# Strassen form for one batch more, work moved between batches, and weight loads reordered, in a fused attention and feed-forward kernel

## The chip, the cores and the metric

One core of one Trainium2 chip. The metric is device time in microseconds (us); a time below is the median of several executions, with the lowest and highest in brackets. Executions whose granted TensorE clock and length mark them as slow are left out of every ratio. TensorE multiplies matrices; VectorE, ScalarE and GpSimd work on vectors. In the profile they are PE, DVE, ACT and POOL. SBUF and PSUM are memories on the chip: in this program TensorE's results go into banks of PSUM, and a bank is copied out before TensorE uses it again.

## The reference, cut to what matters

```
x: 8 batches, 8 heads, 512 rows, 64 wide      state: 8, 8, 32, 64
a     = softmax(x state^T / 8);   xread = a state
a2    = softmax(state x^T / 8);   sread = a2 x
y     = concat(xread, sread), heads side by side       # 8 x 544 rows of 512
h     = y @ w_in                                       # 512 -> 2048
g     = 0.5 h (1 + erf(h / sqrt 2))
out   = g @ w_out                                      # 2048 -> 512
```

The last two products, 512 rows per batch, are nearly all of the time. For the rows of xread the kernel never forms y: it folds state and w_in into one matrix P per batch, so that h = a P.

## The kernel before

First, batch by batch, TensorE forms P (`p_mm`), the first product (`mm1`, called through `M`) and the second. The second has two forms. The plain one (`mm2`, through `U`, and `mm2_m`) is 64 matmuls of 512 columns. The Strassen form (`X`) is seven products of 16 matmuls of 256 columns, and it needs sums of quarters of w_out, made once, and sums of quarters of g, made per batch. Before the change batches 0 and 1 take the plain form.

```
def p_mm(b, f, tiles):                  # one quarter of P, two PSUM banks
    ps = [tiles([128, 512], "p_ps") for t in range(2)]
    ...
def p_copy(b, f, ps):
    nc.scalar.copy(out=dst[:, 0, :], in_=ps[0])
    nc.vector.tensor_copy(out=dst[:, 1, :], in_=ps[1])

def evac(ps, rows):                     # an output tile leaves its bank
    nc.vector.tensor_copy(out=osb, in_=ps)
    ...
```

Second, VectorE's operations with two inputs in SBUF: the multiply that normalises the softmax, the sums of w_out and the sums of g.

```
    nc.vector.tensor_tensor(out=A.a[...], in0=e4, in1=ics[...], op=ALU.mult)      # norm
    nc.vector.tensor_tensor(out=w_sum[name], in0=x, in1=y, op=op)                # w_add
    nc.vector.tensor_tensor(out=t, in0=g_q(b, h0, k0), in1=g_q(b, h1, k1), op=op) # g_sum
```

Third, the weights come in four chunks each of w_in and w_out, counted from 0. After the first ones the queue holds, in this order, w_out 1, w_in 2, w_out 2, w_in 3, w_out 3, and then x of the later batches.

The softmax here doesn't subtract the row's maximum and nothing guards it: scores larger than these inputs give would overflow.

Of the kernel before, what the change touches and what calls it, by code (L numbers as in the profile page):

```python
# [17 lines left out]
def kernel(  # L18
# [8 lines left out]
    nc = tc.nc  # L27

    B, H, S, D = x.shape
    _, _, NS, _ = state.shape  # L30
# [6 lines left out]
    FC = d_ff // 512  # L37
# [41 lines left out]
    hold = persist.tile([128, 1], BF16, name="hold")  # L79
# [23 lines left out]
    def load_w_in(f0, f1):  # L103
        for t in range(2):
            nc.gpsimd.dma_start(
                out=w_in_bf[64 * t:64 * t + 64, :, f0:f1],
                in_=moe_w_in[256 * t:256 * t + 256, f0:f1].rearrange("(c d) f -> d c f", c=HC),
            )
# [3 lines left out]
    def load_w_out(i):  # L112
        nc.gpsimd.dma_start(out=w_out_bf[:, 4 * i:4 * i + 4, :], in_=w_out_r[:, 4 * i:4 * i + 4, :])

    def load_x(b):
        xb = xin.tile([128, H, SJ * D], BF16, name="xb", tag="xb")
        nc.gpsimd.dma_start(out=xb, in_=xr[b])
        xbs[b] = xb
# [12 lines left out]


    def load_rest():
        load_w_out(1)
        for f in range(2, FC):
            load_w_in(512 * f, 512 * f + 512)
            load_w_out(f)
        load_st(2, B)
        load_x(2)
        load_x(3)  # L140


# [80 lines left out]
    def rearr_ones(b):  # L223
        A = atts[b]
        eng = nc.vector if b < 2 else nc.gpsimd
        src = xbs[b].rearrange("p (t c) (j d) -> p t c j d", t=2, d=D)
        for t in range(2):
            eng.tensor_copy(  # L228
                out=A.xo[:, :, :, 2 + 64 * t:66 + 64 * t].rearrange("p j c d -> p c j d"),
                in_=src[:, t],  # L230
            )
# [122 lines left out]
    def atr(b, ts=(0, 1)):  # L354
        A = atts[b]
        if 0 in ts:
            A.AT = att.tile([128, SJ, 2, 128], BF16, name="AT", tag="AT")
        for t in ts:
            ps = ps_f.tile([128, SJ, 128], BF16, name="aT_ps", tag="f")
            for j in range(SJ):  # L360
                nc.tensor.transpose(ps[:, j, :], A.a[:, 2 * j + t, :], ident)
            nc.vector.tensor_copy(out=A.AT[:, :, t, :], in_=ps)
# [36 lines left out]
    def srt(b):  # L399
        A = atts[b]  # L400
        ps = ps_f.tile([128, HC, NS], BF16, name="srT", tag="f")
        nc.tensor.transpose(
            ps.rearrange("p c n -> p (c n)"), A.srm.rearrange("q t d -> q (t d)"), ident
        )
        nc.vector.tensor_copy(out=XSR[:, :, :, b], in_=ps)
# [3 lines left out]
    def p_mm(b, f, tiles):  # L409
        if b not in Ps:  # L410
            Ps[b] = att.tile([128, 2, d_ff], BF16, name="P", tag="P")
        ps = [tiles([128, 512], "p_ps") for t in range(2)]
        for c in range(HC):
            for t in range(2):
                nc.tensor.matmul(  # L415
                    ps[t][32 * c:32 * c + 32, :],
                    lhsT=sbd[64 * t:64 * t + 64, b, c, 32 * t:32 * t + 32],
                    rhs=w_in_bf[64 * t:64 * t + 64, c, f * 512:(f + 1) * 512],
                    start=True,
                    stop=True,  # L420
                )
        return ps

    def p_copy(b, f, ps):
        dst = Ps[b][:, :, f * 512:(f + 1) * 512]
        nc.scalar.copy(out=dst[:, 0, :], in_=ps[0])  # L426
        nc.vector.tensor_copy(out=dst[:, 1, :], in_=ps[1])  # L427

    def pmat(b, f):
        p_copy(b, f, p_mm(b, f, ftile))  # L430



# [1 line left out]
    def burst(chunks, b_read=None):  # L435
        done = []
        first = len(chunks) < 4 and b_read is not None
        if first:
            sread(b_read)
        for i, (b, f) in enumerate(chunks):  # L440
            done.append((b, f, p_mm(b, f, ftile if i < 2 else otile)))
        for x in done[:2]:
            p_copy(*x)
        if b_read is not None and not first:
            sread(b_read)
        for x in done[2:3]:
            p_copy(*x)
        if b_read is not None:
            sread_out(b_read)
        for x in done[3:]:  # L450
            p_copy(*x)
# [19 lines left out]
    gs = {}  # L471
# [73 lines left out]
    def mm2_m(b, m):  # L545
        for j in range(SJ):
            if m == 0:
                ops[b, j] = otile([128, d_model], "op")
            nc.tensor.matmul(  # L549
                ops[b, j],  # L550
                lhsT=gs[b][:, m, j * 128:(j + 1) * 128],
                rhs=w_out_bf[:, m, :],
                start=(m == 0),
                stop=(m == MC - 1),
            )
# [5 lines left out]
    w_sum = {}  # L561

    def w_add(name, x, y, op):
        if name == "3":
            pair = persist.tile([128, 2, MH, NH], BF16, name="ws_34", tag="mix0")
            w_sum["3"], w_sum["4"] = pair[:, 0], pair[:, 1]
        elif name != "4":
            tag = {"6": "mix1", "1": "mix2", "7": "mix3"}[name]
            w_sum[name] = persist.tile([128, MH, NH], BF16, name=f"ws_{name}", tag=tag)
        nc.vector.tensor_tensor(out=w_sum[name], in0=x, in1=y, op=op)  # L570

    def w_sums(i):
        (b11, b12), (b21, b22) = w_q
# [120 lines left out]
    def M(*ms):  # L694
        for m in ms:
            mm1(m // MC, m % MC)

    def U(*us):
        for u in us:
            mm2(u // 16, u % 16 // 4, u % 4)  # L700
# [69 lines left out]
    scores(1, 0)  # L770
    scores(1, 1)
    srt(0)
    U(4, 5)
    rearr_ones(1)
    U(6)
    pmat(0, 2)
    norm(1, 0)
    norm(1, 1)
    U(7)
# [1 line left out]
    sread(1)  # L781
    sread_out(1)
    M(10, 11)
    mm2_m(0, 8)
    mm2_m(0, 9)
    burst([(0, 3), (1, 0)])
    mm2_m(0, 10)
    atr(1)
    M(12, 13)
    srt(1)  # L790
    M(14, 15)
    mm2_m(0, 11)
    begin(2)
    rearr(2)
    xtr_dma(2)
    rearr_ones(2)
    U(12)
    burst([(1, 1), (1, 2)])
    U(13)
    state_prep(2, B)  # L800
    M(16, 17)
    U(14)
    M(18, 19)
    U(15)
    burst([(1, 3), (2, 0), (2, 1)])
    U(16)


    u = 17
    for p in range(2, 8):  # L810
        if p == 4:
            scores(2, 0)
            scores(2, 1)
            norm(2, 0)
            norm(2, 1)
        if p == 7:
            atr_dma(2)
        if p == 3:
            begin(3)
            rearr(3)  # L820
            xtr_dma(3)
            rearr_ones(3)
        M(16 + 2 * p, 17 + 2 * p)
        U(u)
        u += 1
        if p in (5, 7):
            pmat(2, 2 + p // 7)
        if p >= 3:
            w_sums(p - 3)
        if p == 2:  # L830
            nc.gpsimd.tensor_copy(out=hold, in_=gs[1][:, 4, 0:1])
            load_x(4)

    for b in range(2, B):
        nb = b + 1
        for p in range(8):
            k = 16 * b + 2 * p
            if p == 1 and nb < B:
                scores(nb, 0)
                scores(nb, 1)  # L840
            if p in (2, 3) and nb < B:
                norm(nb, p - 2)
            if p == 3 and nb + 1 < B:
                xtr_dma(nb + 1)
            if p == 5 and nb < B:
                atr_dma(nb)
            M(k, k + 1)
            if p == 2:
                srt(b)
            if nb == B and p >= 4:  # L850
                for m in range(4 * p - 16, 4 * p - 12):
                    mm1_sr(m)
            if b == 2:
                for _ in range(2 if p < 4 else 1):
                    if u < 32:
                        U(u)
                        u += 1
            elif p < 5:
                if p == 0:
                    g_sum(b - 1, "5")  # L860
                X(b - 1, "45127"[p])
                if p < 3:
                    g_sum(b - 1, "127"[p])
            if p == 1:
                sread(b)
                sread_out(b)
            if p == 0 and b + 3 < B:
                nc.gpsimd.tensor_copy(out=hold, in_=gs[b][:, 0, 0:1])  # L868
                load_x(b + 3)
            if p == 0 and nb + 1 < B:  # L870
                begin(nb + 1)
                rearr(nb + 1)
            if p == 2 and nb + 1 < B:
                rearr_ones(nb + 1)
            if p == 5:
                g_sum(b, "6")
                if nb < B:
                    p_run(nb, (0, 1), ((0, 1), (3, 2)))
            if p == 6:
                X(b, "3")  # L880
            if p == 7:
                if nb < B:
                    p_run(nb, (2, 3), ((1, 2), None))
                X(b, "6")
# [46 lines left out]
```

## Time and profile before

| | before |
|---|---|
| time | 212.62 us (212.35 to 212.8) |
| profiled span | 211.0 us |
| TensorE busy | 201.6 us, 96% |
| first product of batch 2 starts | 55.68 us |
| first product of batch 3 starts | 76.17 us |

The two starts serve as milestones: all of the change lies before the second one. In timelines each line has start, length, engine, source line, operation, output<-inputs, and in brackets the idle time before it and what ended that. These are the milestones, and the row of the page that gives the granted TensorE clock in 40 slices of the span (9 is full). The clock never drops.

```profile
55.68 1.04 PE L478 MATMUL hp<-AT,P 128*128 128x512 bf16 x4
...
76.17 1.03 PE L478 MATMUL hp<-AT,P 128*128 128x512 bf16 x4
```
```profile
PEclk9999999999999999999999999999999999999999
```

### The profile page before, as it was taken

How to read it: one execution, taken by the hardware profiler on the slowest of the kernel's cores; microseconds unless marked ns; L12 is line 12 of the kernel's file. 1: busy time of each engine (PE TensorE's matmuls, PEld its weight loads, DVE VectorE, ACT ScalarE, POOL GpSimd, SP SyncE). 2: the span in 40 equal slices, each digit the busy share in tenths (PEclk: the TensorE clock that was granted, in tenths of full speed). 3: DMA queues.
4: the chain of work that ended last, by engine and by line, in shares of the span. 5: the costliest groups of instructions: out<-in, count | busy, mean ns of one | idle time of the engine just before them, and what ended most of it. 6: DMA issues, size and time to landing. Idle time of an engine off the chain costs nothing.

```text
span 211.0 us, 4598 instructions
## 1 busy us (share of the span) xinstructions
PE 201.6 (96%) x1929; PEld 128.8 (61%) x1939; DVE 133.6 (63%) x206; ACT 131.2 (62%) x237; POOL 64.1 (30%) x71
## 2 busy tenths in 40 slices
PE   7899999998999999999999999999999999999991
PEld 7645444443454576766675677567766778786860
DVE  2934575748829549984899658955875571324521
ACT  3864775679794779467947596678758455860110
POOL 8954302573171025610566007200230022000320
PEclk9999999999999999999999999999999999999999
DMA  6999999779274909355872910160007001300314
GB/s 201 189 170 204 206 194 186 158 173 179 50 99 102 249 0 127 77 199 53 111 90 122 198 31 3 57 193 3 2 22 230 3 0 47 155 0 0 103 68 132
DMA packets 37861, 23.14 MB, mean 110 GB/s; under 512 B 21712, under 2 KB 35280, under 8 KB 37840
## 3 DMA queue, kind: packets, MB, share of 16 engines
q0 software_dynamic: 13936, 8.10, 28.0%
q1 hardware_dynamic: 23216, 14.29, 27.6%
q10 hardware_dynamic: 688, 0.46, 0.7%
q8 instruction: 15, 0.25, 0.5%
q14 instruction: 6, 0.05, 0.1%
HBM read 17.30 MB, written 8.91 MB: 124 GB/s over the span
## 4 chain that ended last, share of the span: by engine, by line
PE 79%; DMA 10%; DVE 5%; ACT 3%; issue 1%; POOL 0%; ACTq 0%
PE xp L602 32%; PE hp L478 22%; PE op L504 9%; DMA w_out_bf<-in_moe_w_out_dram 6%; PE p_ps L415 4%; DVE gsum L596 3%; PE hps L519 3%; PE ops L531 3%; DMA AT<-a 3%; PE op L549 2%; DMA st_f<-in_state_dram 2%; PE sr L378 1%; PE xT_ps L250 1%; PE pt L324 1%; ACT g L485 1%; DVE s L645 1%
## 5 line engine op out<-in xcount | busy, mean ns | idle before, releaser
L485 ACT ACTIVATE g<-hp 128x512 bf16<-128x512 f32 x124 | 67.5, 603 | 33.7 <-PE hp L478 28.6
L478 PE MATMUL hp<-AT,P 128*128 128x512 bf16 x248 | 63.9, 380 | 0.3
L602 PEld LDWEIGHTS <-gsum 128*128 128x128 bf16 x480 | 46.3, 98 | 11.0 <-issue 2.1
L596 DVE TENSOR_TENSOR gsum<-g 128x2048 bf16<-128x2048 bf16 x30 | 40.0, 1349 | 7.9 <-ACT g L485 6.8
L478 PEld LDWEIGHTS <-P 128*128 128x128 bf16 x248 | 22.4, 98 | 20.7 <-issue 2.6
L602 PE MATMUL xp<-ws,gsum 128*128 128x256 bf16 x288 | 34.4, 273 | 0.0
L427 DVE CAST P<-p_ps 128x512 bf16<-128x512 f32 x31 | 20.0, 684 | 17.2 <-PE p_ps L415 17.2
L650 POOL TENSOR_TENSOR u<-s,oh 128x512 f32<-128x512 f32 x6 | 8.0, 1329 | 67.8 <-ACT oh L648 67.8
L504 PE MATMUL op<-w_out_bf,g 128*128 128x512 bf16 x90 | 23.0, 379 | 0.6 <-DMA w_out_bf<-in_moe_w_out_dram 0.4
L602 PE MATMUL xp<-ws,g 128*128 128x256 bf16 x192 | 22.9, 273 | 0.0
L602 PE MATMUL xp<-w_out_bf,gsum 128*128 128x256 bf16 x192 | 22.9, 273 | 0.0
L426 ACT CAST P<-p_ps 128x512 bf16<-128x512 f32 x31 | 17.0, 604 | 7.4 <-PE p_ps L415 7.4
L602 PEld LDWEIGHTS <-g 128*128 128x128 bf16 x192 | 18.8, 98 | 4.3
L504 PEld LDWEIGHTS <-g 128*128 128x128 bf16 x96 | 9.1, 98 | 11.8 <-issue 1.6
L218 POOL COPY x<-xb 128x1024 bf16<-128x1024 bf16 x12 | 12.6, 1082 | 10.9 <-DMA xb<-in_x_dram 10.9
L347 DVE TENSOR_TENSOR a<-e,ics 128x512 bf16<-128x512 bf16 x14 | 15.1, 1078 | 0.5
L228 POOL COPY xo<-xb 128x1024 bf16<-128x1024 bf16 x12 | 13.5, 1157 | 1.3 <-PE sr L378 1.3
L645 DVE TENSOR_TENSOR s<-xp,s 128x512 f32<-128x512 f32 x6 | 4.2, 692 | 14.5 <-PE xp L602 14.5
L621 POOL TENSOR_TENSOR v<-q,oh 128x512 f32<-128x512 f32 x6 | 8.0, 1326 | 15.8 <-ACT oh L652 13.8
L344 DVE TENSOR_REDUCE cs<-e 128x16 f32<-128x512 bf16 x14 | 9.5, 677 | 3.8 <-ACT e L331 3.8
L415 PE MATMUL p_ps<-w_in_bf,sbd 64*32 64x512 bf16 x248 | 11.0, 383 | 0.8 <-ACT g L485 0.7
L868 POOL COPY hold<-g 128x1 bf16<-128x1 bf16 x3 | 1.0, 330 | 31.0 <-ACT g L485 31.0
(91 smaller groups left out, 208.4 us busy)
## 6 DMA issues: line engine op xcount, KB each, us to landing
out_dram<-oh SPq DMA_DIRECT2D x11, 512.0 KB, 2.7
xb<-in_x_dram POOLq DMA_DIRECT2D x7, 512.0 KB, 6.9
out_dram<-osb SPq DMA_DIRECT2D x9, 256.0 KB, 3.3
w_out_bf<-in_moe_w_out_dram POOLq DMA_DIRECT2D x4, 512.0 KB, 12.6
w_in_bf<-in_moe_w_in_dram POOLq DMA_DIRECT2D x6, 256.0 KB, 12.2
x0f<-in_x_dram SPq DMA_DIRECT2D x3, 256.0 KB, 4.0
w_in_bf<-in_moe_w_in_dram POOLq DMA_DIRECT2D x4, 128.0 KB, 3.9
x0f<-in_x_dram ACTq DMA_DIRECT2D x1, 256.0 KB, 4.4
```

What stands on the lines that cost most here:

```text
L218: nc.gpsimd.tensor_copy(out=A.x4[:, :, :, 64 * t:64 * t + 64].rearrange("p j c d -> p c j d"), in_=src[:, t],)
L228: eng.tensor_copy(out=A.xo[:, :, :, 2 + 64 * t:66 + 64 * t].rearrange("p j c d -> p c j d"), in_=src[:, t],)
L344: nc.vector.reduce_sum(out=cs, in_=e4, axis=AX.X)
L347: nc.vector.tensor_tensor(out=A.a[:, :, hs].rearrange("p g (c n) -> p g c n", n=NS), in0=e4, in1=ics[:, :, :].to_broadcast((128, G, 2, NS) ...
L415: nc.tensor.matmul(ps[t][32 * c:32 * c + 32, :], lhsT=sbd[64 * t:64 * t + 64, b, c, 32 * t:32 * t + 32], rhs=w_in_bf[64 * t:64 * t + 64, c ...
L426: nc.scalar.copy(out=dst[:, 0, :], in_=ps[0])
L427: nc.vector.tensor_copy(out=dst[:, 1, :], in_=ps[1])
L478: nc.tensor.matmul(hp, lhsT=Ps[b][:, t, m * 128:(m + 1) * 128], rhs=atts[b].AT[:, :, t, :], start=(t == 0), stop=(t == 1),)
L485: nc.scalar.activation(out=gs[b][:, m, :], in_=hp, func=AF.Gelu)
L504: nc.tensor.matmul(ps, lhsT=gs[b][:, m, j * 128:(j + 1) * 128], rhs=w_out_bf[:, m, :], start=(m == 0), stop=(m == MC - 1),)
L596: nc.vector.tensor_tensor(out=t, in0=g_q(b, h0, k0), in1=g_q(b, h1, k1), op=op)
L602: nc.tensor.matmul(ps[:, j - js[0], :], lhsT=lhs[:, m, 128 * j:128 * j + 128], rhs=rhs[:, m, :], start=(first and j == js[0] and m == 0), ...
```

## The change

Its intent: give batch 1 the cheaper Strassen form; fill the gaps that this leaves by moving half of batch 0's second product back among batch 1's first; and bring w_in one chunk ahead of w_out. With more sums to make on VectorE, three of the five sums of w_out go to GpSimd. Batch 0's third P product also moves ahead of three steps of its second product, with both of its copies on VectorE. The core of the diff (`atr` transposes the normalised attention on TensorE, `atr_dma` by DMA; `srt` transposes sread):

```
 def load_rest():
+    load_w_in(1024, 1536)
     load_w_out(1)
-    for f in range(2, FC): load_w_in(512 * f, 512 * f + 512); load_w_out(f)
+    load_w_in(1536, 2048)
+    load_w_out(2)
     load_st(2, B); load_x(2)
+    load_w_out(3)
     load_x(3)
 def w_add(name, x, y, op):
+    eng = nc.vector if name in "36" else nc.gpsimd
-    nc.vector.tensor_tensor(out=w_sum[name], in0=x, in1=y, op=op)
+    eng.tensor_tensor(out=w_sum[name], in0=x, in1=y, op=op)
 ... (the stretch around batch 1 is written anew; its end:)
+    scores(2, 0); scores(2, 1)
+    w_sums(0); w_sums(1)               # "3" on VectorE, "4" on GpSimd
+    nc.gpsimd.tensor_copy(out=hold, in_=gs[1][:, 4, 0:1]); load_x(4)
+    M(24, 25)
+    U(14)
+    norm(2, 0); norm(2, 1)
+    U(15)                              # its output copy is behind both norms
+    w_sums(2); w_sums(3); w_sums(4)    # "6" on VectorE, "1" and "7" on GpSimd
+    M(26, 27)
+    g_sum(1, "6")
+    p_run(2, (0, 1), ((0, 1), (3, 2))) # P in the banks of batch 0's output
+    M(28, 29); X(1, "3"); M(30, 31)
+    atr(2)                             # was atr_dma(2)
+    p_run(2, (2, 3), ((1, 2), None))
+    X(1, "6")
 for b in range(2, B): ...
+    if p == 3: srt(b)
     M(k, k + 1)
-    if p == 2: srt(b)
-    if b == 2: U(...)                  # batch 1's plain second product
+    if p < 5: ... X(b - 1, "45127"[p])
```

More of the change, by code (lines that the diff above doesn't have):

```diff
@@ L133, in load_rest @@
     def load_rest():
+        load_w_in(1024, 1536)
         load_w_out(1)
-        for f in range(2, FC):
-            load_w_in(512 * f, 512 * f + 512)
-            load_w_out(f)
+        load_w_in(1536, 2048)
+        load_w_out(2)
         load_st(2, B)
         load_x(2)
+        load_w_out(3)
         load_x(3)
@@ L422, in p_mm, with p_copy, pmat @@
         return ps
-    def p_copy(b, f, ps):
+    def p_copy(b, f, ps, first=None):
         dst = Ps[b][:, :, f * 512:(f + 1) * 512]
-        nc.scalar.copy(out=dst[:, 0, :], in_=ps[0])
+        (first or nc.scalar.copy)(out=dst[:, 0, :], in_=ps[0])
         nc.vector.tensor_copy(out=dst[:, 1, :], in_=ps[1])
-    def pmat(b, f):
-        p_copy(b, f, p_mm(b, f, ftile))
+    def pmat(b, f, first=None):
+        p_copy(b, f, p_mm(b, f, ftile), first)
     def burst(chunks, b_read=None):
@@ L772 @@
     srt(0)
+    pmat(0, 2, nc.vector.tensor_copy)
     U(4, 5)
@@ L775 @@
     U(6)
-    pmat(0, 2)
     norm(1, 0)
@@ L783 @@
     M(10, 11)
+    burst([(0, 3), (1, 0)])
+    M(12, 13)
+    atr(1)
+    M(14, 15)
     mm2_m(0, 8)
+    srt(1)
     mm2_m(0, 9)
-    burst([(0, 3), (1, 0)])
-    mm2_m(0, 10)
-    atr(1)
-    M(12, 13)
-    srt(1)
-    M(14, 15)
-    mm2_m(0, 11)
+    burst([(1, 1), (1, 2)])
     begin(2)
@@ L796 @@
     rearr_ones(2)
+    M(16, 17)
+    mm2_m(0, 10)
+    M(18, 19)
+    mm2_m(0, 11)
+    state_prep(2, B)
+    pmat(1, 3)
+    begin(3)
+    rearr(3)
+    xtr_dma(3)
+    rearr_ones(3)
+    M(20, 21)
     U(12)
-    burst([(1, 1), (1, 2)])
+    M(22, 23)
     U(13)
-    state_prep(2, B)
-    M(16, 17)
+    scores(2, 0)
+    scores(2, 1)
+    w_sums(0)
+    w_sums(1)
+    nc.gpsimd.tensor_copy(out=hold, in_=gs[1][:, 4, 0:1])
+    load_x(4)
+    M(24, 25)
     U(14)
-    M(18, 19)
+    norm(2, 0)
+    norm(2, 1)
     U(15)
-    burst([(1, 3), (2, 0), (2, 1)])
-    U(16)
-    u = 17
-    for p in range(2, 8):
-        if p == 4:
-            scores(2, 0)
-            scores(2, 1)
-            norm(2, 0)
-            norm(2, 1)
-        if p == 7:
-            atr_dma(2)
-        if p == 3:
-            begin(3)
-            rearr(3)
-            xtr_dma(3)
-            rearr_ones(3)
-        M(16 + 2 * p, 17 + 2 * p)
-        U(u)
-        u += 1
-        if p in (5, 7):
-            pmat(2, 2 + p // 7)
-        if p >= 3:
-            w_sums(p - 3)
-        if p == 2:
-            nc.gpsimd.tensor_copy(out=hold, in_=gs[1][:, 4, 0:1])
-            load_x(4)
+    w_sums(2)
+    w_sums(3)
+    w_sums(4)
+    M(26, 27)
+    g_sum(1, "6")
+    p_run(2, (0, 1), ((0, 1), (3, 2)))
+    M(28, 29)
+    X(1, "3")
+    M(30, 31)
+    atr(2)
+    p_run(2, (2, 3), ((1, 2), None))
+    X(1, "6")
     for b in range(2, B):
@@ L846 @@
                 atr_dma(nb)
+            if p == 3:
+                srt(b)
             M(k, k + 1)
-            if p == 2:
-                srt(b)
             if nb == B and p >= 4:
@@ L852 @@
                     mm1_sr(m)
-            if b == 2:
-                for _ in range(2 if p < 4 else 1):
-                    if u < 32:
-                        U(u)
-                        u += 1
-            elif p < 5:
+            if p < 5:
                 if p == 0:
```

## The prediction

> **What bounds the kernel now.** I read the page first (busy time, then the chain), then TensorE in order of time, then the waits, then VectorE and GpSimd side by side.
>
> ```profile
> PE 201.6 (96%) x1929; PEld 128.8 (61%) x1939; DVE 133.6 (63%) x206; ACT 131.2 (62%) x237; POOL 64.1 (30%) x71
> PE 79%; DMA 10%; DVE 5%; ACT 3%; issue 1%; POOL 0%; ACTq 0%
> ```
>
> TensorE sets the time: 96% busy, so of 211.0 us only 9.4 are open, of which about 1 lies at the start and about 4 after the last matmul. What another order can win is therefore small. The waits of TensorE, all of them:
>
> ```profile
> PE srT L402 <- DVE srm L392: 0.8, 2, 0.4
> PE p_ps L415 <- ACT g L485: 0.7, 1, 0.7
> PE aT_ps L361 <- POOL a L309: 0.5, 1, 0.5
> PE op L504 <- DMA w_out_bf<-in_moe_w_out_dram: 0.4, 1, 0.4
> PE op L549 <- DMA w_out_bf<-in_moe_w_out_dram: 0.3, 1, 0.3
> ```
>
> The loads are barely ahead early on. In the timeline (start, length, engine, line, idle before in brackets) the second chunk of w_out is met as it lands, and the piece of the chain below gives its landing, 10.16 + 11.90 = 22.06. By the issue-to-landing times of their line, the two halves of w_in's third chunk (issued from 10.97) land at about 22.8 and 24.2.
>
> ```profile
> 10.16 11.90 DMA w_out_bf<-in_moe_w_out_dram
> 22.10 2.75 PE L504 MATMUL op<-w_out_bf,g 128*128 128x512 bf16 x11 [0.36 <-DMA w_out_bf<-in_moe_w_out_dram]
> 24.78 0.41 PE L415 MATMUL p_ps<-w_in_bf,sbd 64*32 64x512 bf16 x8
> 25.12 1.04 PE L504 MATMUL op<-w_out_bf,g 128*128 128x512 bf16 x4
> ```
>
> Most telling for this change is VectorE beside GpSimd. The same multiply (softmax normalisation, both inputs in SBUF) takes 0.69 us while GpSimd rests and 1.45 to 1.57 us while it works:
>
> ```profile
> 50.96 0.69 DVE L347 TENSOR_TENSOR a<-e,ics 128x512 bf16<-128x512 bf16 x1
> 83.33 1.26 POOL L650 TENSOR_TENSOR u<-s,oh 128x512 f32<-128x512 f32 x1 [2.31 <-ACT oh L648]
> 84.55 2.49 POOL L228 COPY xo<-xb 128x1024 bf16<-128x1024 bf16 x2
> 84.56 1.57 DVE L347 TENSOR_TENSOR a<-e,ics 128x512 bf16<-128x512 bf16 x1
> 88.99 1.27 POOL L621 TENSOR_TENSOR v<-q,oh 128x512 f32<-128x512 f32 x1 [1.96 <-ACT oh L652]
> 89.36 1.45 DVE L347 TENSOR_TENSOR a<-e,ics 128x512 bf16<-128x512 bf16 x1
> ```
>
> The last pair shows the size of it: GpSimd ends at 90.26, the multiply at 90.81, so it ran only about 0.6 us after GpSimd let go.
>
> **What the Trainium skill says.** "SBUF — State Buffer", section "Who interferes with whom": a VectorE instruction with two SBUF inputs and a GpSimd instruction that reads SBUF exclude each other, the second waiting until the first has finished. The trace agrees, up to the 1.27 us of its longest GpSimd arithmetic. "GPSIMD Engine Reference", section 3.1: tensor_tensor on GpSimd costs about 2.6 cycles per element. At that page's 1.2 GHz, 512 elements are 1.1 us; the trace has 1.27 for u. "TensorE: Matmul & The Clock Gate", Part 1: after some 3.4 us of idling TensorE runs at half clock until it has been busy as long again. No wait in this trace is long enough to show that.
>
> **The change, part by part.**
>
> *Strassen for batch 1.* Removed: 64 matmuls of 512 columns. From start to start the trace has 0.864 us per four (24.78 to 26.00 less the 0.34 of the eight small ones), so 13.8 us. Added: 112 matmuls of 256 columns, 1.745 us per 16 (the chain has 1.75), so 12.2. Gain 1.6. But the transpose of batch 2's attention moves from the DMA queue to TensorE: eight transposes, +0.45 (31.48 to 31.93). Net -1.2 us on TensorE.
>
> *Old waits that go.* The srT transposes move behind a Strassen product: two waits, 0.8 us, gone. The copy that frees their PSUM bank now stands behind a later normalisation, which may return some; I count -0.5. The 0.7 us wait on ScalarE, plus slack around it (TensorE advances by less than its work between 47 and 52), and the 0.36 on w_out sit in stretches I rebuild below; from 22.1 to the first product of batch 3 (76.17) I count about 1.6 us idle before.
>
> *Loads.* w_in chunk 3 and w_out chunk 2 only swap places in a queue that is never empty there, so their sum lands at the same 24.15. TensorE now does the small products of w_in's chunk first (21.7 to about 22.5) and then needs w_out: it waits from about 22.5 to 24.2, **+1.7**. Later chunks are early enough.
>
> *Back to back.* Batch 1's first product now follows the P bursts with nothing between; it must wait for the copies of P out of PSUM (0.6 to 0.7 us each on ScalarE and VectorE). Three such places, about **+1.3** together.
>
> *A bank held by VectorE.* The built program shows that the second P product of batch 2 needs the bank of batch 0's last output tile, and the copy that empties it stands on VectorE behind both normalisations of batch 2. I estimate that TensorE is there at about 48.2 to 48.6. The normalisations can't start before the exponentials: scores at 44.2, and in the trace 2.4 us from the scores to the first reduction, then the output copy in front, so 47.1. In the trace both take 48.35 to 51.57, 3.2 us; plus 0.6 for the copy gives 51. So even with GpSimd at rest: **+2.5**.
>
> *Three weight sums to GpSimd.* Each is 128x2048, on VectorE 1.22 us. On GpSimd I scale u: 4 x 1.27 = 5 at most, and the page's 2.6 cycles give 4.4; I use 4.4. They stand in a row, 13 us, from when x of batch 3 has been loaded and rearranged, which my count of the loads puts at about 43, until about 58. In just that stretch VectorE has five operations with two SBUF inputs to do, in order: sum 3, two normalising multiplies, sum 6, the first difference of g. Sum 3, ready at 44.9, waits to 47; done 48.3. Then osb copy, reduction, reciprocal (1.6 us together) and the multiply meets GpSimd's second sum, which started at about 49.7: it waits to 54.2. The second multiply meets the third sum: to 58.6 or 59.3. Only then is the bank emptied, at about 60. If the first multiply wins its race (both come within 0.3 us of each other) the bank is free at 56, but sum 6 then waits out the third GpSimd sum and the P copies behind it come as late as 63. Either way batch 2's first product starts at about 66.5, not 57.8 as without the exclusion: **+8.5**. A wait that long would also cool the clock: an estimate from the page, 3.4 us at half rate, is **+1.7**.
>
> Sum: without exclusion -1.2 - 1.6 - 0.5 + 1.7 + 1.3 + 2.5 = +2.2, with some 0.5 for later copies +2.7: **215.3**. With it +2.7 + 8.5 + 1.7 = +12.9: **225.5**. After batch 2 both kernels run the same stages and nothing is won back, as TensorE is full there.
>
> **Rivals.**
> 1. *The mild one:* GpSimd yields inside a long instruction, or its sums run earlier, and only the bank wait and the load wait remain: 213 to 217. For it: the trace shows the exclusion only with instructions of up to 1.3 us. Against it: at every overlap I looked at, the multiply ended as though it had begun when GpSimd ended.
> 2. *The intended one:* order and loads fit, all waits in the early stretch vanish. TensorE's 1.2 us, 1.6 us of old waits and 0.5 of srT are all there is: 209.3. Against it: the load wait and the bank wait follow from the program's order and from landings that the trace gives. For it: someone who moves so many things presumably looked at where they fell.
> 3. *The harsh one:* exclusion, a cold clock, and delays that carry into batch 2's VectorE work, where three more differences of g queue: 226 to 229.
>
> **Range and chances.** I hold the exclusion more likely than not (about 0.6), and the mild and intended cases 0.4 together, so my number lies between the modes, nearer the upper one: 221.5. The range spans both: 212.5 to 228. More than 2% faster would need 4.3 us where at most 3.3 are to be had: 0.03. Slower by over 2% is above 216.9: 0.59. Within: 0.38.
>
> **What would show it.** TensorE's waits: one on w_out near 22 of about 1.7 us (loads); one of a P product of batch 2 on VectorE's output copy near 48, 2.5 us (mild) or 8 to 12 (exclusion). On VectorE: the L347 multiply of batch 2 (a line or so further down) at several us each, and the sum beside it, ending where a GpSimd sum ends; 0.69 each would refute the exclusion. On GpSimd: three tensor_tensor of 4 to 5 us. The granted clock just after the wait shows the cooling. The prediction fails if GpSimd's sums take 2 us, or if they come before or after VectorE's chain.

## The result, and the profile after

The changed kernel takes 225.72 us (224.93 to 226.56, four runs) against 212.71 us (212.35 to 213.52) of the kernel before on the same chip: 13.0 us slower. The ratio is 1.061 (95% interval 1.055 to 1.066). Ratios here are the mean time of one kernel's fast runs over that of the other's in the same rounds, so not quite the ratio of the medians.

The profiled span is 224.3 us. Three views say where the time went. The page's busy line, chain and clock row:

```profile
PE 203.3 (91%) x1989; PEld 134.8 (60%) x1995; DVE 147.3 (66%) x211; ACT 132.7 (59%) x239; POOL 79.9 (36%) x76
PEclk9999999997589999999999999999999999999999
PE 61%; DVE 23%; DMA 10%; issue 2%; POOL 1%; ACT 1%; SPq 0%; DVEq 0%
```

VectorE's share of the chain that ended last is 23%, where it was 5%, and the clock has a hole near a quarter of the span. TensorE's waits (total, times, longest):

```profile
PE p_ps L416 <- DVE osb L492: 10.7, 1, 10.7
...
PE op L505 <- DMA w_out_bf<-in_moe_w_out_dram: 0.8, 1, 0.8
...
PE p_ps L416 <- DVE XSR L406: 0.4, 1, 0.4
```

One wait of 10.7 us is most of the loss of 13.0. Now TensorE in order of time, at the load wait and around the long one:

```profile
22.39 0.41 PE L416 MATMUL p_ps<-w_in_bf,sbd 64*32 64x512 bf16 x7 [0.43 <-DVE XSR L406]
23.63 3.61 PE L505 MATMUL op<-w_out_bf,g 128*128 128x512 bf16 x15 [0.83 <-DMA w_out_bf<-in_moe_w_out_dram]
...
59.56 0.62 PE L416 MATMUL p_ps<-w_in_bf,sbd 64*32 64x512 bf16 x7 [10.73 <-DVE osb L492]
60.12 1.89 PE L479 MATMUL hp<-AT,P 128*128 128x512 bf16 x4
61.80 2.57 PE L604 MATMUL xp<-ws,g 128*128 128x256 bf16 x16
64.21 1.03 PE L479 MATMUL hp<-AT,P 128*128 128x512 bf16 x4
...
68.13 1.03 PE L479 MATMUL hp<-AT,P 128*128 128x512 bf16 x4
...
90.26 1.03 PE L479 MATMUL hp<-AT,P 128*128 128x512 bf16 x4
```

The second P product of batch 2 waits from 48.83 to 59.56 for an output copy on VectorE. Then four matmuls take 1.68 us from start to start (0.864 at full rate) and the Strassen product behind them 2.41 (1.745): the clock was cold, at a cost of about 1.5 us. Batch 2 starts at 68.13, 12.45 later than before; batch 3 at 90.26, 14.09 later. From there to the end 134.0 us pass against 134.8. What held VectorE is seen beside GpSimd:

```profile
44.89 2.88 DVE L572 TENSOR_TENSOR ws<-w_out_bf 128x2048 bf16<-128x2048 bf16 x1
...
49.28 8.02 DVE L348 TENSOR_TENSOR a<-e,ics 128x512 bf16<-128x512 bf16 x1
...
58.22 0.69 DVE L348 TENSOR_TENSOR a<-e,ics 128x512 bf16<-128x512 bf16 x1
58.83 0.68 DVE L492 COPY osb<-op 128x512 f32<-128x512 f32 x1
```
```profile
42.62 4.06 POOL L572 TENSOR_TENSOR ws<-w_out_bf 128x2048 bf16<-128x2048 bf16 x1
46.63 1.18 POOL L816 COPY hold<-g 128x1 bf16<-128x1 bf16 x1
47.75 0.91 POOL L117 DMA_DIRECT2D xb<-in_x_dram  x1
48.68 8.06 POOL L572 TENSOR_TENSOR ws<-w_out_bf 128x2048 bf16<-128x2048 bf16 x2
```

GpSimd's first sum ends at 46.68, and VectorE's sum 3, waiting since 44.89, ends 1.09 later, which is about its own length. In that time GpSimd's copy of one column takes 1.18 instead of 0.18: here GpSimd waited for VectorE. Then the multiply waits through both of GpSimd's next sums: they end at 56.74, the multiply at 57.30. The second multiply, with GpSimd at rest, takes 0.69.

### The profile page after: what moved, and what is told of

It reads as the page before. It is cut to its first block, busy times and chain, and to the rows that moved or that the text cites. A ratio compares the mean times of both kernels' runs of the same rounds, so it can differ in the third digit from the quotient of the medians.

```text
span 224.3 us, 4723 instructions
## 1 busy us (share of the span) xinstructions
PE 203.3 (91%) x1989; PEld 134.8 (60%) x1995; DVE 147.3 (66%) x211; ACT 132.7 (59%) x239; POOL 79.9 (36%) x76
## 3 DMA queue, kind: packets, MB, share of 16 engines
HBM read 17.30 MB, written 8.91 MB: 117 GB/s over the span
## 4 chain that ended last, share of the span: by engine, by line
PE 61%; DVE 23%; DMA 10%; issue 2%; POOL 1%; ACT 1%; SPq 0%; DVEq 0%
PE xp L604 28%; PE hp L479 17%; DVE gsum L598 7%; DVE a L348 7%; DMA w_out_bf<-in_moe_w_out_dram 5%; PE p_ps L416 4%; PE hps L520 3%; PE ops L532 3%; DMA AT<-a 3%; PE op L505 2%; DVE cs L345 2%; DMA x0f<-in_x_dram 2%; PE op L550 2%; DVE ws L572 1%; DVE ics L347 1%
## 5 line engine op out<-in xcount | busy, mean ns | idle before, releaser
L604 PEld LDWEIGHTS <-gsum 128*128 128x128 bf16 x560 | 54.3, 98 | 13.9 <-issue 2.3
L598 DVE TENSOR_TENSOR gsum<-g 128x2048 bf16<-128x2048 bf16 x35 | 46.8, 1353 | 7.9 <-ACT g L486 6.8
L604 PE MATMUL xp<-ws,gsum 128*128 128x256 bf16 x336 | 40.2, 273 | 0.0
L604 PE MATMUL xp<-ws,g 128*128 128x256 bf16 x224 | 27.4, 277 | 0.0
L604 PE MATMUL xp<-w_out_bf,gsum 128*128 128x256 bf16 x224 | 26.7, 273 | 0.0
L604 PEld LDWEIGHTS <-g 128*128 128x128 bf16 x224 | 22.3, 100 | 5.7 <-issue 0.5
L427 ACT CAST P<-p_ps 128x512 bf16<-128x512 f32 x30 | 16.5, 601 | 13.9 <-PE p_ps L416 13.8
L416 PE MATMUL p_ps<-w_in_bf,sbd 64*32 64x512 bf16 x248 | 12.8, 389 | 11.3 <-DVE osb L492 10.7
L348 DVE TENSOR_TENSOR a<-e,ics 128x512 bf16<-128x512 bf16 x14 | 22.5, 1605 | 0.5
L416 PEld LDWEIGHTS <-sbd 64*32 64x32 bf16 x248 | 3.1, 89 | 20.7 <-issue 20.4
L572 POOL TENSOR_TENSOR ws<-w_out_bf 128x2048 bf16<-128x2048 bf16 x3 | 12.1, 4054 | 0.0
L654 ACT COPY oh<-xp 128x512 f32<-128x512 f32 x7 | 4.1, 587 | 10.0 <-PE xp L604 4.0
```

Source lines behind the costliest of these rows:

```text
L348: nc.vector.tensor_tensor(out=A.a[:, :, hs].rearrange("p g (c n) -> p g c n", n=NS), in0=e4, in1=ics[:, :, :].to_broadcast((128, G, 2, NS) ...
L416: nc.tensor.matmul(ps[t][32 * c:32 * c + 32, :], lhsT=sbd[64 * t:64 * t + 64, b, c, 32 * t:32 * t + 32], rhs=w_in_bf[64 * t:64 * t + 64, c ...
L427: (first or nc.scalar.copy)(out=dst[:, 0, :], in_=ps[0])
L572: eng.tensor_tensor(out=w_sum[name], in0=x, in1=y, op=op)
L604: nc.tensor.matmul(ps[:, j - js[0], :], lhsT=lhs[:, m, 128 * j:128 * j + 128], rhs=rhs[:, m, :], start=(first and j == js[0] and m == 0), ...
```

## The experiments

The theory: most of the loss is VectorE shut out while GpSimd's sums run (called the exclusion), reaching TensorE through the output copy behind the multiplies; the rest is the bank wait that is there anyway, the cold clock and the load wait. The main rivals: the order on VectorE alone causes it, or the early loads do. There were twelve runs of eleven kernels, all with correct results.

**sums_vector: all five sums on VectorE.**

```
-        eng = nc.vector if name in "36" else nc.gpsimd
+        eng = nc.vector
```

> The changed kernel with all five weight sums on VectorE, nothing else. Theory (exclusion between GpSimd's long sums and VectorE's two-input work): the 8 us multiply falls back to 0.69 us, the wait of the P product on the output copy shrinks from 10.7 to about 3 us (the order of VectorE's program alone), a second wait of about 1.5 us appears at the next P products because the copies of P stand behind three more sums; batch 2's first product starts at about 60 instead of 68.1, total about 217.5. Rival (the order of the copy alone, GpSimd innocent): VectorE gets more work, so the wait does not shrink and the time stays at 225 or grows.

Measured: 218.97 us (217.95 to 220.83), ratio 1.030 (1.023 to 1.036). Having the three sums on GpSimd rather than on VectorE therefore costs about 6.8 of the 13.0 us, by the medians. The first multiply (the second took 0.69 too) and the copy behind them on VectorE, then TensorE's waits:

```profile
50.83 0.69 DVE L348 TENSOR_TENSOR a<-e,ics 128x512 bf16<-128x512 bf16 x1
...
53.05 0.68 DVE L492 COPY osb<-op 128x512 f32<-128x512 f32 x1
```
```profile
PE p_ps L416 <- DVE osb L492: 3.0, 1, 3.0
PE op L550 <- DMA w_out_bf<-in_moe_w_out_dram: 1.4, 1, 1.4
PE op L505 <- DMA w_out_bf<-in_moe_w_out_dram: 1.2, 1, 1.2
...
PE p_ps L416 <- DVE P L428: 0.9, 2, 0.7
```

The bank wait without exclusion is 3.0 us, so 7.7 of the 10.7 are exclusion, and the clock stays full. But the kernel is still 6 us slower than before: the loads are met later in this execution (1.4 and 1.2 on w_out), and P's copy now stands behind sums on VectorE (0.9).

**copy_first: the output copy ahead of the multiplies, sums as in the change.**

```
     U(14)
+    U(15)
     norm(2, 0)
     norm(2, 1)
-    U(15)
```

> The changed kernel with batch 0's last output tile finished before the two normalisations of batch 2, so that the bank is emptied at about 49; the three sums stay on GpSimd. Theory: the wait on the output copy is gone, but the multiply still lasts about 8 us, so TensorE only does some 5 us of work more and then waits for the normalised attention (about 5 us) and for the copies of P (about 2.5 us): total 222.5 to 223.5. Rival (order of the copy alone): the 10.7 us go, total about 215.

Measured: 224.42 us (223.87 to 224.73), ratio 1.054 (1.051 to 1.057). The wait on the copy was to vanish and is 7.07. This time sum 3, which stands ahead of the copy, was the one shut out:

```profile
46.31 10.01 DVE L572 TENSOR_TENSOR ws<-w_out_bf 128x2048 bf16<-128x2048 bf16 x1
56.24 1.27 DVE L492 COPY osb<-op 128x512 f32<-128x512 f32 x2
```
```profile
46.23 0.92 POOL L117 DMA_DIRECT2D xb<-in_x_dram  x1
47.16 8.07 POOL L572 TENSOR_TENSOR ws<-w_out_bf 128x2048 bf16<-128x2048 bf16 x2
```

So the rival of order alone falls: here again one two-input operation of VectorE paid for GpSimd's whole run. Sum 3 begins in the record 0.85 us before GpSimd's next sums do, and loses all the same. Nothing else in the record shows why.

**both: both edits at once.**

```
-        eng = nc.vector if name in "36" else nc.gpsimd
+        eng = nc.vector
...
     U(14)
+    U(15)
     norm(2, 0)
     norm(2, 1)
-    U(15)
```

> Both edits at once. Theory: no wait on the output copy, both multiplies 0.69 us; but the copies of P stand behind five sums on VectorE, so the later P products wait about 3 us: about 217.5, no better than the sums on VectorE alone. Rival (the two causes add up independently): the sum of both gains, about 214.5.

Measured: 219.88 us over four runs; one (221.88, also the profiled one) counts as slow, the fast ones gave 217.4, 219.67 and 220.1, ratio 1.029 (1.022 to 1.036). No better than sums_vector: with the exclusion gone, the order on VectorE only moves the wait to the next copy of P (2.71 us in the profiled run).

**sums_cut and sums_cut2: GpSimd's sums in four pieces each; the same kernel twice.**

```
-        eng.tensor_tensor(out=w_sum[name], in0=x, in1=y, op=op)
+        for m in range(0, MH, MH if eng is nc.vector else 2):
+            n = slice(m, m + (MH if eng is nc.vector else 2))
+            eng.tensor_tensor(out=w_sum[name][:, n], in0=x[:, n], in1=y[:, n], op=op)
```

> The changed kernel with each of the three GpSimd sums cut into four instructions of 512 columns, about 1.1 us each, the same total work on GpSimd. If VectorE is let in between two GpSimd instructions (as a multiply of the kernel before was between two copies): each multiply waits at most about 1.1 us, total about 219. If a queue of GpSimd instructions keeps the door shut (as the multiply of the changed kernel waited through two sums on end): the multiply lasts 8 us or more still, total 225 to 227.

> The same kernel as sums_cut, once more, because its runs fell into two groups (218 and 227) and only one of the 218 was traced. If VectorE's turn between two of GpSimd's pieces is chance, some runs again lie near 218 and some near 227, with nothing in between. A traced run near 227 should have one operation of VectorE with two SBUF inputs that lasts 8 us or more, and TensorE waiting for what follows it; a run near 218 none over 3 us. If instead 227 was a slow state of the chip, all its stages are longer and no such operation is there.

Measured, first time: 217.98, 218.62, 227.15 and 226.86 us, the latter two at clock 0.976. Second time: all four at 227.79 to 229.66, ratio 1.072 (1.069 to 1.076), clock 0.968. A run of each kind was traced. The first, at 217.98:

```profile
46.77 1.22 DVE L574 TENSOR_TENSOR ws<-w_out_bf 128x2048 bf16<-128x2048 bf16 x1
...
49.96 0.70 DVE L348 TENSOR_TENSOR a<-e,ics 128x512 bf16<-128x512 bf16 x1
```
```profile
46.72 0.91 POOL L117 DMA_DIRECT2D xb<-in_x_dram  x1
47.65 12.04 POOL L574 TENSOR_TENSOR ws<-w_out_bf 128x512 bf16<-128x512 bf16 x8
```

The second, at 229.66:

```profile
48.49 10.18 DVE L574 TENSOR_TENSOR ws<-w_out_bf 128x2048 bf16<-128x2048 bf16 x1
```
```profile
47.74 0.92 POOL L117 DMA_DIRECT2D xb<-in_x_dram  x1
48.68 8.91 POOL L574 TENSOR_TENSOR ws<-w_out_bf 128x512 bf16<-128x512 bf16 x8
```

In the first, VectorE takes turns with the pieces: the two operations shown have their own length, the two that follow are lengthened by at most 1 us (sum 6 takes 1.57 and the difference of g 2.17, where 1.22 is usual), and GpSimd's eight pieces stretch to 12.04 us. In the second the eight pieces run through in 8.91 and VectorE's sum waits for all of them, though there are seven ends of an instruction in between. The second group is thus the exclusion again, at least where it was traced. Cutting GpSimd's work is no remedy. In both traces the sum begins while GpSimd issues a load, 0.05 us into it in the first and 0.75 in the second; but in copy_first it begins 0.08 us into it and loses, so this moment alone doesn't decide. What decides the hand-over stays open; a fixed rule that VectorE is let in at the next end of a GpSimd instruction is refuted.

**warm_fill and warm_fill2: TensorE kept busy on zeros during the long wait** (190 and 140 matmuls of 128 columns).

```
             done.append((b, f, p_mm(b, f, tiles)))
+            if (b, f) == (2, 0):
+                wp = ftile([128, 512], "wp")
+                for _ in range(190):       # warm_fill2: 140
+                    nc.tensor.matmul(wp[:, 0:128], lhsT=warm, rhs=warm, start=True, stop=True)
```

> The changed kernel with 190 small matmuls on a zero tile (about 56 ns each, 10.6 us) put where TensorE waits for the output copy. The wait's end is set by VectorE and stays at about 59.6. Theory (the wait also cools the clock): the four matmuls and the first product after it run at full rate, 0.86 and 1.75 us instead of 1.68 and 2.41, so 1.4 us less: about 224.3, ratio 1.054. Rival (they are slow because they wait for something): no change, 225.7, or slower if the filler overruns.

> The changed kernel with 140 small matmuls on zeros in place of 190 put into TensorE's long wait, so that they end before the bank comes free. The filler's matmuls took 57 ns each, so about 8 us, ending near 58. Theory (the cold clock alone costs about 1.5 us of the loss): TensorE stays at full rate, the product after the wait takes 1.74 and not 2.41, and the total falls to about 224.2, ratio 1.050 to 1.056 against 1.0606 of the changed kernel. Rival (what the warm clock wins is lost in a later wait): 225.5 or more, ratio 1.058 up.

Measured: warm_fill 226.12 us (224.41 to 226.73), ratio 1.060: no gain. The filler ended at about 60.9, and the copy that frees the bank had ended at 59.85 in the same execution, so it ate what the warm clock won. warm_fill2: 224.36 us median, ratio 1.052 (1.049 to 1.055); one of its four runs (233.09) was slow and is left out. The shorter filler ends in time, and TensorE goes on at full rate: four matmuls in 0.87 and the product in 1.75.

```profile
48.95 7.98 PE L695 MATMUL wp<-warm 128*128 128x128 bf16 x140
...
59.61 0.41 PE L416 MATMUL p_ps<-w_in_bf,sbd 64*32 64x512 bf16 x7 [2.36 <-DVE osb L492]
59.95 1.04 PE L479 MATMUL hp<-AT,P 128*128 128x512 bf16 x4
60.82 1.91 PE L604 MATMUL xp<-ws,g 128*128 128x256 bf16 x16
62.57 1.03 PE L479 MATMUL hp<-AT,P 128*128 128x512 bf16 x4
```

From the end of the wait to the start of the third group it takes 2.96 us here and 4.65 in the changed kernel. The clock's share of the loss is thus 1.5 to 1.7 us (the medians differ by 1.4), and it follows from the wait.

**early_old: sums on VectorE, and the loads and the third P chunk of batch 0 in their old places.**

```
-        load_w_in(1024, 1536)
         load_w_out(1)
-        load_w_in(1536, 2048)
-        load_w_out(2)
+        for f in range(2, FC): load_w_in(512 * f, 512 * f + 512); load_w_out(f)
...
-        load_w_out(3)
...
-    pmat(0, 2, nc.vector.tensor_copy)
...
     U(6)
+    pmat(0, 2)
```

> The changed kernel with all sums on VectorE (that run took 218.97, ratio 1.030), and the loads and batch 0's third P product in the order of the kernel before. If the load order by itself costs: the wait of 1.2 us on w_out and its clock drops go, ratio about 1.020. If the wait only moves: TensorE then meets the next P products at about 28 us before the last chunk of w_in has landed (29.7 in the kernel before) and waits some 1.4 us there: ratio 1.027 to 1.033.

Measured: 216.94 us (216.63 to 218.09), ratio 1.020 (1.016 to 1.023), against 1.030 (1.023 to 1.036) of sums_vector: the new order of the loads, with the P product that moved along, costs about 2 us of the whole. The run itself is classed as unclear against 2%, and the two runs, on different chips, have intervals that nearly touch. Some 4 us are left that no edit of the changed kernel removed. The old order doesn't save all of it, as the moved bursts now meet w_in (1.1 us of waits).

**srt_only: the kernel before with nothing changed but the place of srt.**

```
-            M(k, k + 1)
-            if p == 2: srt(b)
+            if p == 3: srt(b)
+            M(k, k + 1)
```

> The kernel before with only the srT transposes of batches 2 to 7 moved behind the next Strassen product. Theory: the two waits (0.8 us) go, up to 0.6 us come back as waits for the bank that VectorE then empties later: 212.1 to 212.6, ratio 0.996 to 1.000. If the new waits were larger than the old: above 1.000.

Measured: 212.66 us (212.08 to 213.16), ratio 0.998 (0.995 to 1.001): the two waits on srT are gone and 0.4 us come back on the copy of its result. Not told apart from nothing.

**best_a, best_b and best_c: the kernel before with the Strassen form for batch 1 and all sums on VectorE, in three orders.** All keep the old early part and loads; best_a and best_b transpose batch 2's attention by DMA, best_c on TensorE.

```
 best_a                        best_b                          best_c
 w_sums(0); w_sums(2)          w_sums(0); w_sums(2)            w_sums(0); w_sums(2)
 ...                           ...                             ... x of batch 3 rearranged
 w_sums(1)                     burst([(1,3),(2,0),(2,1)])      burst([(1,3),(2,0),(2,1)])
 burst([(1,3),(2,0),(2,1)])    U(14)                           U(14)
 ... x of batch 3 rearranged   ... x of batch 3 rearranged     ...
 U(14)                         w_sums(1)                       M(22,23); scores(2)
 M(22,23); scores(2); U(15)    M(22,23); scores(2)             norm(2); g_sum(1,"6")
 g_sum(1,"6"); w_sums(3)       norm(2); g_sum(1,"6")           M(24,25); X(1,"3")
 M(24,25); norm(2); X(1,"3")   M(24,25); U(15)                 M(26,27); U(15)
 M(26,27); pmat(2,2)           M(26,27); X(1,"3")              atr(2); pmat(2,2)
 w_sums(4); atr_dma(2)         pmat(2,2); w_sums(3)            w_sums(1); w_sums(3)
 M(28,29); X(1,"6")            atr_dma(2); M(28,29)            M(28,29); X(1,"6")
                               w_sums(4); X(1,"6")             w_sums(4)
```

> The kernel before up to its first product of batch 1, the Strassen form for batch 1 from there, all five sums on VectorE in places where it idled (after the last load of w_out, at about 33 and 40 us), only two of batch 0's output steps moved back, the old load order, the transpose of batch 2 again by DMA. Theory: TensorE's 1.6 us less work and half of the srT waits come through because nothing new is waited for: 210.0 to 211.5, ratio about 0.99. Rival (ScalarE becomes the bound in that stretch, with two table loads and 12 activations and fewer products to cover them): 212.5 to 214.

> The kernel before with only the Strassen form for batch 1, all weight sums on VectorE, both halves of the second product moved back, and the order of best_a mended at the places where its trace had waits: the normalisations of batch 2 stand directly behind their scores, ahead of the difference of g; sum 4 behind them; the copies of P ahead of any sum. Theory (the waits of best_a, 1.4 on the transposed attention, 0.7 on P's copy, 0.6 on g, come from that order): about 211, ratio 0.988 to 0.996. Rival (the form has no room for its sums and differences without waits): 213 to 215, ratio 1.00 to 1.01. Nothing over 2% either way.

> best_b mended at its three waits: the loads of batch 3's x are rearranged by GpSimd earlier, so that they no longer hold up a normalising multiply (1.88 us there); the transposes of batch 2's attention on TensorE in place of the DMA (its wait was 1.6), with the second block of the second product between; sum 1 behind the normalisations. Theory (order alone is at fault): the waits of 1.6, 1.2 and 0.5 go, TensorE does 0.45 more: about 212.2, ratio 0.994 to 1.000. Rival (each mended place opens another wait): 213.5 to 215, ratio 1.003 to 1.010.

Measured: best_a 214.54 us, ratio 1.008 (1.004 to 1.012); best_b 214.98, ratio 1.009 (1.006 to 1.013); best_c 213.54, ratio 1.004 (1.000 to 1.008). The gain was missed each time, and each time other waits stood there. TensorE's waits in best_b, then in best_c:

```profile
PE hp L478 <- DMA AT<-a: 1.6, 1, 1.6
PE xp L602 <- DVE gsum L596: 1.2, 1, 1.2
```
```profile
PE aT_ps L361 <- ACT s L640: 1.2, 1, 1.2
```

In best_c this wait and one of 0.69 us behind it were followed by a cold clock: the share granted from 52 to 54 us is 0.50, and the work behind is as slow as in the changed kernel, at a cost of about 1.5 us.

```profile
49.06 0.62 PE L361 MATMUL aT_ps<-ident,a 128*128 128x128 bf16 x8 [1.19 <-ACT s L640]
51.16 1.87 PE L478 MATMUL hp<-AT,P 128*128 128x512 bf16 x4 [0.69 <-ACT P L426]
52.82 2.57 PE L602 MATMUL xp<-ws,gsum 128*128 128x256 bf16 x16
```

Three of best_c's six runs show a mean clock of 0.988 to 0.990 and took 213.8 to 214.8 us; the other three (0.997 or more) took 212.9 to 213.3, still no less than the kernel before (212.0 to 213.9). The Strassen form does save work: TensorE was busy 201.1 us in best_a and 202.3 in srt_only, 1.2 less, with as many matmul records as weight loads in both. But in all three orders new waits were worth more than that. None of the twelve runs is shown to beat the kernel before.

## Why the prediction was right or wrong

The direction was right, slower by over 2%, and the time lies in the range; but the stated 221.5 is 4.2 us below the 225.7 measured, and the sum for the case with exclusion, 225.5, is what came. By its steps:

- *The choice between the cases* is where the number went wrong. It was put between a mild and an exclusion mode with 0.4 and 0.6. For the changed kernel all four executions lie at 224.9 to 226.6, none in the mild mode. The bimodality exists, but in the kernel with cut sums (218 and 227 to 230). The argument that the trace shows the exclusion only for instructions up to 1.3 us was no ground for doubt: an instruction of 4.06 us held just as well.
- *Exclusion, +8.5*: the mechanism was right and the size near: 7.7 of the wait. Its course was not as told. The first multiply was to wait for one sum and the second for the next; in fact the first waited for both. The end was about the same, the bank free at 59.5 where 60 was predicted. The sums took 4.06 us where 4.4 were reckoned. (The prediction's own starts, 66.5 less 57.8, give 8.7 and not 8.5.)
- *The bank, +2.5*: 3.0 us in sums_vector.
- *Cold clock, +1.7*: 1.5 to 1.7.
- *Load wait, +1.7*: 0.83 for w_out, which was there by 23.63 and not 24.2; with 0.43 just before it, for a bank that a copy on VectorE frees, 1.26. *Back to back, +1.3*: 0.8 (0.48 and 0.16 for copies of P, 0.15 for a bank).
- *TensorE's work, -1.2, old waits, -1.6, and srT, -0.5*: srT gave about 0.4 net by its waits. Of the Strassen form's 1.6 us about 1.2 shows in busy time. The prediction's 13.8 for the plain form rests on 0.864 per four, where the lines that the prediction cites give 0.88 (24.78 to 26.00 less 0.34); 0.86 is what most other places have. Its list of TensorE's waits also leaves out the largest, 1.0 us before the first warm-up matmul, which the change doesn't touch.
- *The sum without exclusion, 215.3*, was too low: sums_vector, the nearest experiment, takes 219.0. Its extra is in larger load waits (2.6 in its profile, where the changed kernel's had 0.8) and in the copies of P behind the sums. Conversely, exclusion and cold clock were to cost 10.2, and putting the sums back on VectorE wins only 6.8, net of the waits that they make there. So part of the hit at 225.5 is luck, two errors that cancel. The terms that I could measure (10.7 of bank and exclusion, 1.5 of clock, 1.3 and 0.8 of the other new waits, less 1.4 that TensorE idled in the kernel before between 22.0 and 76.17, 0.4 of srT and 0.8 of work, which is 1.2 less the 0.45 of the transposes) add to some 11.7 us of the 13.0; the rest is spread over pauses that I could not put down to single causes.

The harsh rival, 226 to 229 with delays that carry on, didn't occur: after batch 3's start the kernel is 0.8 us quicker than before. The intended rival, 209.3, was not reached even with the exclusion and the new loads taken out (best_c, 213.5).

## What to carry to other kernels

Before work is moved from a busy VectorE to an idle GpSimd, look at which two-input VectorE operations fall in its stretch and what waits behind them: three sums of 1.2 us each, moved to take them off VectorE, held it for 8 us and made a wait of TensorE of 3.0 us into one of 10.7. When an engine is 96% busy, a rewrite that saves 1.2 us of its work has to bring in no new wait at all; count the waits that each new place can open before counting the gain. And when a number is formed by weighing two modes, say so, and expect to land on one of them.

## What the Trainium skill lacked or had wrong

- "SBUF — State Buffer", "Who interferes with whom", says that the order of issue decides who blocks. These traces agree with the exclusion, but the page doesn't say how that order can be read from a trace, and the order of the recorded starts is not it: in copy_first VectorE's sum began at 46.31, GpSimd's next sum at 47.16, and VectorE's came second, after 10.01 us.
- The same section doesn't say who wins at the end of an instruction when GpSimd has its next one ready. In the changed kernel VectorE was let in behind the first sum (GpSimd's copy then took 1.18 us for 0.18), and then shut out through two sums in a row (8.02 us). With eight pieces in a row it was let in between them in one execution and shut out through all eight in another (10.18 us).
- "TensorE: Matmul & The Clock Gate", Part 1, ties the cold clock to some 3.4 us of idling. The 10.73 us wait agrees. But a cold clock followed far shorter pauses too: in best_c waits of 1.19 and 0.69 us, after which the granted clock is 0.50 from 52 to 54 us and four matmuls took 1.66 us for 0.86; in sums_cut, at 217.98 us, one of 0.43 and one of 1.15, and 0.50 from 24 to 26. In sums_vector 0.44 and 1.23 us at the same place were not followed by it. What decides stays open.
